# Talking-heads attention and two feed-forward layers: softmax statistics for two chunks at a time, one pair of heads of values and scores in every step, and 64-column scores

## The chip, the cores and the metric

One core of a Trainium2 chip. The time is device microseconds of one execution. An execution under the profiler gives a trace besides, with its span: from the first to the last instruction of the program.

## What is computed

Talking-heads attention over 2 batches, 12 heads, 448 positions and 64 features, then two gated feed-forward layers over the 896 tokens, all in float32:

```python
scores = scale * np.matmul(q, k.transpose(0, 1, 3, 2))
scores = np.einsum('bhij,hg->bgij', scores, w_pre)
scores = scores - np.max(scores, axis=-1, keepdims=True)
attn = np.exp(scores)
attn = attn / (np.sum(attn, axis=-1, keepdims=True) + 1e-09)
attn = np.einsum('bhij,hg->bgij', attn, w_post)
return np.matmul(attn, v).astype(np.float32)
...
g = x @ w_gate
silu = g * (1.0 / (1.0 + np.exp(-g)))
val = x @ w_val
return (silu * val @ w_out).astype(np.float32)
...
h = x @ w_in
relu6 = np.clip(h + 3.0, 0.0, 6.0)
g = h * relu6 / 6.0
return (g @ w_out).astype(np.float32)
```

The heads are mixed before the softmax (`w_pre`) and after it (`w_post`).

## The kernel before

The attention is cut into 8 tiles `t` of queries, 4 for each batch (`TILES`, lines 34 to 37), and each tile into chunks of 10 queries: 12, 12, 12, 9, 11, 12, 12 and 10 chunks, 90 in all. A step `i` of the main loop (lines 553 to 585, 45 steps) works on two chunks. Since the stages of a chunk pair run in different steps, each step issues work of several pairs.

- `scores` (line 154) makes the scores of one pair of heads for a whole tile, with the queries as the stationary operand in two groups of rows: 64 and the rest. The rest is `n - 64`, with `n` ten times the number of chunks: 56 columns for 12 chunks, 46 for 11, 36 for 10, and 26 for tile 3, which has 9. Each of the two heads gets a PSUM bank of the tag `pqk`, which has two. `scores_out` (line 177) copies them into one of two score buffers in SBUF, `Ss[t % 2]`. `qk` (line 500) is both.
- `relayout` and `relayout_rest` (lines 186 and 201) move the score rows of a chunk, by DMA, into a tile `sx` in which the heads lie on partitions. The large part is issued on SP's queue, the small one on POOL's. A pool of 5 holds `sx`. A tile's rows can be moved when all six pairs of heads of that tile have been copied, and its score buffer can be written again when all of its rows have been read.
- `premix` (line 210) mixes the heads of two chunks on TensorE, 8 instructions, into two banks of the tag `ppre`, which has four. It runs two steps ahead (`LOOK`).
- `row_max`, `exps` and `weights` (lines 228 to 246) work on one chunk each: the negated maximum of each row on VectorE; the exponential with its row sum on ScalarE; the sum plus 1e-9, its reciprocal, and `w_post` times the reciprocal on VectorE.
- `postmix` (line 248) mixes the heads again on TensorE, 64 instructions for two chunks, into the two banks of the tag `ppost`. `attn_out` (line 269) copies one bank with VectorE and the other with ScalarE into `at`.
- `av` (line 287) multiplies one pair of heads of a tile with the values, in one `pqk` bank. `x_out` (line 308) copies it into a staging tile; for tiles 6 and 7 `x_last` (line 328) casts it on ScalarE and subtracts on VectorE. `x_split` runs on POOL.

The order of the work is written out by hand; each engine executes its instructions in that order. Lines 506 to 509 place the scores of tiles 2 to 7: tile 2 in steps 2 to 7, tile 3 in 8 to 13, tile 4 in 13 to 17 (two in step 13), then 19 to 24, 24 to 29, 30 to 35. Lines 512 to 518 place `av`, two pairs of heads in one step, three such steps for each tile. Before the loop the scores of tiles 0 and 1 are made. Weights of the first two feed-forward products are loaded and converted during steps 20 to 35 on ScalarE and VectorE, and begun on TensorE in the last steps (`fill`).

A step issues, in this order: `postmix(i)`; both `exps` of pair `i + 1`; `attn_out(i)`; `weights` of its first chunk; the scores of this step and their copies; `weights` of its second chunk; `premix(i + 2)` and both `row_max`; `av`; and `x_out` with loads, conversions and relayouts.

After the loop come the six `av` of tile 7 (line 587), which take banks of `ppre` and `ppost` in turn, and the feed-forward layers (lines 654 to 670): 52 pairs of PSUM banks, given out in a fixed rotation (`BANKS`, line 341).

## Time and profile before

| | |
|---|---|
| median of 3 runs | 710.16 us (709.96 to 710.25) |
| span of the profiled execution | 712.3 us |
| TensorE matmuls busy | 679.8 us (95%) |
| VectorE busy | 517.3 us (73%) |
| ScalarE busy | 303.1 us (43%) |
| GpSimd busy | 147.9 us (21%) |

The span is 2.1 us above the median; no time of its own is given for the profiled execution. Busy is the union of an engine's instructions. PE is TensorE, DVE VectorE, ACT ScalarE, POOL GpSimd, SP the queue that issues most DMAs; L259 is line 259 of the kernel. The ends of matmuls are modelled, and one may be drawn as long while it waits. Steps can be found in the trace by their `postmix`: step 9 starts at 57.10 us, 13 at 78.88, 14 at 85.89, 36 at 174.93 and 44 at 203.84. The feed-forward products proper begin at 219.90.

### The profile page before, as it was taken

How to read it: one execution, taken by the hardware profiler on the slowest of the kernel's cores; microseconds unless marked ns; L12 is line 12 of the kernel's file. 1: busy time of each engine (PE TensorE's matmuls, PEld its weight loads, DVE VectorE, ACT ScalarE, POOL GpSimd, SP SyncE). 2: the span in 40 equal slices, each digit the busy share in tenths (PEclk: the TensorE clock that was granted, in tenths of full speed). 3: DMA queues.
4: the chain of work that ended last, by engine and by line, in shares of the span. 5: the costliest groups of instructions: out<-in, count | busy, mean ns of one | idle time of the engine just before them, and what ended most of it. 6: DMA issues, size and time to landing. Idle time of an engine off the chain costs nothing.

```text
span 712.3 us, 16449 instructions
## 1 busy us (share of the span) xinstructions
PE 679.8 (95%) x6864; PEld 570.3 (80%) x6864; DVE 517.3 (73%) x925; ACT 303.1 (43%) x581; POOL 147.9 (21%) x185
## 2 busy tenths in 40 slices
PE   9698899899879999999999999999999999999997
PEld 3353465565569999999999999999999999999997
DVE  4785578899845888888878666568888888764650
ACT  4574566667533424334343322324544544333320
POOL 2422244442420121131112000002332332000000
PEclk9999999999999999999999999999999999999999
DMA  5777346443421424333342334223323323544420
GB/s 193 219 207 210 110 123 193 141 160 100 125 87 46 133 91 133 105 117 114 109 126 97 108 114 133 89 89 94 128 90 95 126 82 97 166 145 144 136 71 27
DMA packets 33628, 86.73 MB, mean 122 GB/s; under 512 B 9265, under 2 KB 21953, under 8 KB 33553
## 3 DMA queue, kind: packets, MB, share of 16 engines
q1 hardware_dynamic: 25632, 80.97, 35.4%
q0 software_dynamic: 7200, 3.94, 2.4%
q8 instruction: 54, 0.88, 0.5%
q10 hardware_dynamic: 720, 0.77, 0.3%
q14 instruction: 22, 0.17, 0.1%
HBM read 62.20 MB, written 2.75 MB: 91 GB/s over the span
## 4 chain that ended last, share of the span: by engine, by line
PE 83%; DVE 8%; DMA 4%; ACT 2%; issue 2%; SPq 0%; POOL 0%; ACTq 0%; DVEq 0%; POOLq 0%
PE pi L394 16%; PE pp L394 16%; PE po L394 12%; PE pg L394 12%; PE pv L394 12%; PE pav L295 4%; PE pqk L166 4%; PE ppost L259 3%; DMA sx<-S 2%; DVE nm L230 2%; PE ppre L217 2%; DVE wn L245 2%; DMA q<-in_q_dram 2%; DVE at L283 1%; ACT e L236 1%
## 5 line engine op out<-in xcount | busy, mean ns | idle before, releaser
L394 PE MATMUL pp<-g,hp 128*128 128x448 f32 x384 | 109.1, 365 | 0.0
L394 PE MATMUL po<-u,ho 128*128 128x448 f32 x288 | 81.7, 364 | 0.0
L259 PEld LDWEIGHTS ppost<-wn,e 60*64 60x64 f32 x2880 | 49.5, 136 | 37.5 <-ACT at L283 12.8
L605 POOL TENSOR_TENSOR g<-rl,g 128x448 fp32r<-128x448 f32 x32 | 41.6, 1319 | 169.0 <-ACT g L604 169.0
L394 PEld LDWEIGHTS pp<-g,hp 128*128 128x128 f32 x384 | 72.0, 187 | 5.8
L236 ACT ACTIVATE e<-ppre,nm 128x448 f32<-128x448 f32 x90 | 56.2, 630 | 47.8 <-DVE nm L230 47.6
L206 POOL DMA_DIRECT2D sx<-S x90 | 52.1, 579 | 110.5 <-ACT S L182 37.2
L259 PE MATMUL ppost<-wn,e 60*64 60x60 f32 x2880 | 55.8, 223 | 16.6 <-DVE rc L242 5.5
L394 PE MATMUL pi<-x2h,li 128*128 128x448 f32 x192 | 70.2, 366 | 0.0
L394 PE MATMUL pi<-x2l,hi 128*128 128x448 f32 x192 | 70.0, 364 | 0.0
L394 PE MATMUL pi<-x2h,hi 128*128 128x448 f32 x192 | 69.9, 364 | 0.0
L394 PE MATMUL pp<-g,lp 128*128 128x448 f32 x192 | 69.3, 361 | 0.0
L605 POOL TENSOR_TENSOR u<-sg,u 128x448 fp32r<-128x448 f32 x24 | 32.6, 1378 | 152.7 <-ACT u L604 152.7
L230 DVE TENSOR_REDUCE nm<-ppre 128x1 f32<-128x448 f32 x90 | 51.7, 616 | 9.0 <-PE ppre L217 9.0
L394 PEld LDWEIGHTS po<-u,ho 128*128 128x128 f32 x288 | 54.1, 188 | 3.8
L166 PE MATMUL pqk<-k,q 64*64 64x448 f32 (+4 forms) x384 | 53.3, 567 | 3.4 <-ACT S L182 1.9
L295 PEld LDWEIGHTS pav<-at,v 128*64 128x64 f32 x768 | 36.9, 137 | 23.4 <-ACT S L182 17.6
L394 PE MATMUL po<-u,lo 128*128 128x448 f32 x144 | 52.3, 363 | 0.0
L394 PE MATMUL pg<-xl,hg 128*128 128x448 f32 x138 | 50.5, 366 | 0.0
L394 PE MATMUL pv<-xl,hv 128*128 128x448 f32 x138 | 50.5, 366 | 0.0
L394 PE MATMUL pg<-xh,hg 128*128 128x448 f32 x138 | 50.5, 366 | 0.0
L394 PE MATMUL pv<-xh,hv 128*128 128x448 f32 x138 | 50.4, 365 | 0.0
(105 smaller groups left out, 1359.3 us busy)
## 6 DMA issues: line engine op xcount, KB each, us to landing
sx<-S SPq DMA_DIRECT2D x90, 182.0 KB
ri<-in_moe_w_in_dram SPq DMA_DIRECT2D x16, 768.0 KB
rg<-in_moe_w_gate_dram SPq DMA_DIRECT2D x12, 768.0 KB
rv<-in_moe_w_val_dram SPq DMA_DIRECT2D x12, 768.0 KB
ro<-in_moe_w_out_dram SPq DMA_DIRECT2D x12, 768.0 KB
rp<-in_moe_w_out_dram SPq DMA_DIRECT2D x12, 640.0 KB
rp<-in_moe_w_out_dram SPq DMA_DIRECT2D x6, 768.0 KB
sx<-S POOLq DMA_DIRECT2D x90, 42.0 KB, 5.0
```

Of the source, the lines that this page charges most:

```text
L166: nc.tensor.matmul(p[e][lo:hi, :S], lhsT=qs[b][r, base + lo : base + hi], rhs=ks[b][r, c, :], start=True, stop=True, tile_position=(64 * e ...
L206: nc.gpsimd.dma_start(out=sx[m // 2][104:128, m % 2, :], in_=rows[8:, :H, :])
L217: nc.tensor.matmul(p[a][64 * r : 64 * r + 64, :S], lhsT=W1[rows, :], rhs=x[rows, r, :], start=True, stop=True, tile_position=(64 * a, 64 * r),
L230: nc.vector.tensor_reduce(nm, pre[m][:, :S], AX.X, ALU.max, negate=True)
L236: nc.scalar.activation(e[:, :S], pre.pop(m)[:, :S], AF.Exp, bias=tot.pop(m), scale=1.0, accum_out=sm)
L245: nc.vector.tensor_scalar(wn, W2, rc, None, ALU.mult)
L259: nc.tensor.matmul(p[s][64 * c : 64 * c + 64, r, b, :, :], lhsT=e[rows, k0 : k0 + 64], rhs=wn[rows, :, :], start=True, stop=True, tile_pos ...
L283: copy(dst, p[r].rearrange("p a b h k -> p a (b h) k"))
L295: nc.tensor.matmul(p[64 * e : 64 * e + 64, :n], lhsT=vs[b][:, jc, h, :], rhs=ats[t][:, jc, h, :n], start=jc == 0, stop=jc == JC - 1, tile_ ...
L394: nc.tensor.matmul(p[:, :S], lhsT=wt[:, kk, :], rhs=xx, start=start, stop=stop)
L605: eng.tensor_tensor(to[1], src, to[0].bitcast(F32), ALU.subtract)
```

## The change

- The two chunks of a pair share one `ppre` tile of two banks. One instruction takes both maxima, one adds 1e-9, one takes both reciprocals, and one tensor-tensor multiply makes the weights of both, with `w_post` and the reciprocals broadcast.
- The scores of tiles 2 to 7 are placed one pair of heads in each of the steps 1 to 36, at the end of the step, after `premix`. `av` comes right after `exps`, one pair of heads in each of the steps 6 to 40 (two in step 18) and six in steps 41 to 44.
- `x_out` runs on ScalarE, between `attn_out` and `weights`. Of the score copies VectorE does the first head's always (before, not for odd pairs from tile 2 on).
- In tile 3 the second group of score rows has 64 columns in place of 26: it reads on into the next queries, 40 zero columns are appended to `q`, and the additional rows are not used.
- The feed-forward layers take pairs of banks in the rotation `pqk`, `ppre`, `ppost`, `ppre`, a `ppre` pair being one tile; the six `av` of tile 7 take `ppost` alone.

```diff
-    BUFS = {"pqk": 2, "ppre": 4, "ppost": 2}
+    BUFS = {"pqk": 2, "ppre": 2, "ppost": 2}
+
+    def two_banks(name, tag):
+        if tag == "ppre":
+            p = ps.tile([128, 2, 512], F32, name=name, tag=tag, bufs=BUFS[tag])
+            return [p[:, a, :] for a in range(2)]
+        return [ps.tile([128, 512], F32, name=f"{name}_{a}", tag=tag, bufs=BUFS[tag]) for a in range(2)]
...
-            lo, hi = 64 * s, min(64 * s + 64, n)
+            lo, hi = 64 * s, 64 * s + (64 if n < 97 else min(64, n - 64 * s))
...
-            copy = nc.scalar.copy if e or (t > 1 and c % 2) else nc.vector.tensor_copy
+            copy = nc.scalar.copy if e else nc.vector.tensor_copy
...
+    def row_max(i):
+        nm = pe.tile([128, 2], F32, name=f"nm{i}", tag="nm", bufs=3)
+        nc.vector.tensor_reduce(nm, pre[i][:, :, :S], AX.X, ALU.max, negate=True)
+        tot[i] = nm
+
+    def exps(i):
+        p, nm = pre.pop(i), tot.pop(i)
+        sm = pe.tile([128, 2], F32, name=f"sm{i}", tag="sm", bufs=3)
+        e2 = [es[(2 * i + a) % 6] for a in range(2)]
         for a in range(2):
...
+            nc.scalar.activation(
+                e2[a][:, :S], p[:, a, :S], AF.Exp, bias=nm[:, a : a + 1], scale=1.0, accum_out=sm[:, a : a + 1]
+            )
+        ew[i] = (e2, sm)
+
+    def weights(i):
+        sm = ew[i][1]
+        rc = pe.tile([128, 2], F32, name=f"rc{i}", tag="rc", bufs=3)
         nc.vector.tensor_scalar(rc, sm, 1e-9, None, ALU.add)
         nc.vector.reciprocal(rc, rc)
...
+        wn = pe.tile([128, 2, GP], F32, name=f"wn{i}", tag="wn", bufs=3)
+        w2 = W2.rearrange("p g k -> p (g k)")
+        nc.vector.tensor_tensor(
+            wn, w2.unsqueeze(1).to_broadcast([128, 2, GP]), rc.unsqueeze(2).to_broadcast([128, 2, GP]), ALU.mult
+        )
...
-        nc.vector.tensor_copy(stage[t][:, c, :n], pavs.pop((t, c))[:, :n])
+        nc.scalar.copy(stage[t][:, c, :n], pavs.pop((t, c))[:, :n])
...
-    for t, (begin, end) in enumerate(((2, 7), (8, 13), (13, 17), (19, 24), (24, 29), (30, 35)), 2):
+    for t in range(2, 8):
         for c in range(HP):
-            at_step(begin + c * (end - begin + 1) // HP, qk, t, c, place="qk")
-        scored[t] = end
+            at_step(6 * t - 11 + c, qk, t, c, place="qk")
+        scored[t] = 6 * t - 6
...
-    for t in range(7):
-        begin = (first[t + 1] - 1) // 2 + 1
-        end = first[t + 2] // 2 - 1 if t < 6 else NP - 1
+    for t, (begin, end) in enumerate(((6, 11), (12, 17), (18, 22), (23, 28), (29, 34), (35, 40), (41, 44))):
         for c in range(HP):
-            i = begin + (c // 2) * (end - begin) // 2
+            i = begin + c * (end - begin + 1) // HP
             at_step(i, av, t, c, place="av")
-            at_step(i, x_out if t < 6 else x_last, t, c)
+            at_step(i, x_out if t < 6 else x_last, t, c, place="out")
...
-        soft = [2 * (i + 1) + a for a in range(2)] if 0 <= i + 1 < NP else []
-        for m in soft:
-            exps(m)
+        soft = 0 <= i + 1 < NP
+        if soft:
+            exps(i + 1)
+        run(i, "av")
         if i >= 0:
             attn_out(i)
-        for m in soft[:1]:
-            weights(m)
-        run(i, "qk")
-        for m in soft[1:]:
-            weights(m)
+        run(i, "out")
+        if soft:
+            weights(i + 1)
         if i + LOOK < NP:
             premix(i + LOOK)
-            for a in range(2):
-                row_max(2 * (i + LOOK) + a)
+            row_max(i + LOOK)
         if i >= NP - 3:
             fill(FILL[i - NP + 3])
-        run(i, "av")
+        run(i, "qk")
...
-        av(7, c, ("ppre", "ppost")[c % 2])
+        av(7, c, "ppost")
...
+        part.append(np.zeros((128, QPAD), q.dtype))
```

## Rows read from the trace of the kernel before

**Rows 1.** Busy time by stretches: stretch, its length, then busy us of each engine.

```profile
65.00:67.19 2.19, 0.07 (x6) 0.05 (x4) 0.58 (x2) 1.34 (x4) 1.14 (x2) 1.00 0.86 228
67.19:70.60 3.41, 3.41 (x28) 0.84 (x28) 1.65 (x7) 0.64 (x1) 1.15 (x2) 0.50 0.84 221
...
85.89:174.93 89.04, 80.45 (x2149) 51.95 (x2141) 75.95 (x239) 59.26 (x147) 34.55 (x56) 1.00 0.47 148
174.93:203.84 28.91, 23.47 (x703) 17.06 (x703) 23.94 (x82) 17.37 (x47) 12.75 (x19) 1.00 0.46 138
203.84:219.90 16.06, 14.07 (x224) 12.35 (x223) 4.45 (x10) 2.38 (x9) 1.80 (x1) 1.00 0.01 2
...
240.00:270.00 30.00, 30.00 (x149) 27.80 (x148) 25.26 (x32) 12.74 (x20) 5.55 (x4) 1.00 0.38 125
```

After the length stand PE, PE's weight loads, DVE, ACT and POOL, then the granted clock, the share of DMA and GB/s.

**Rows 2.** The chain of waits that ended last: start us, us, what.

```profile
78.95 1.09 PE ppost L259 x64
...
163.72 0.48 ACT e L236
164.26 0.81 ACT e L236 x3
165.06 0.53 ACT at L283
165.59 0.40 ACT S L182
166.03 1.75 PE pav L295 x32
```

**Rows 3.** Timeline of TensorE: start us, us, what (steps 9 and 25).

```profile
57.10 1.16 PE L259 MATMUL ppost<-wn,e 60*64 60x60 f32 x64
58.08 1.79 PE L166 MATMUL pqk<-k,q 64*64 64x448 f32 x8
...
132.60 0.93 PE L166 MATMUL pqk<-k,q 64*64 64x448 f32 x8
133.35 0.93 PE L217 MATMUL ppre<-sx,W 64*64 64x448 f32 x8
```

**Rows 4.** Groups of TensorE's score matmuls by form: busy us, mean ns of one.

```profile
L166 PE MATMUL pqk<-k,q 64*26 64x448 f32 x24 | 6.3, 603 | 0.0
...
L166 PE MATMUL pqk<-k,q 64*36 64x448 f32 x24 | 5.5, 535 | 0.0
```

**Rows 5.** Groups of VectorE from 17 to 221 us: busy us, mean ns of one.

```profile
L230 DVE TENSOR_REDUCE nm<-ppre 128x1 f32<-128x448 f32 x90 | 51.7, 616 | 9.0 <-PE ppre L217 9.0
L283 DVE COPY at<-ppost 128x480 f32<-128x480 f32 x45 | 30.1, 670 | 15.0 <-PE ppost L259 15.0
L245 DVE TENSOR_SCALAR wn<-W,rc 128x60 f32<-128x60 f32 x90 | 27.6, 307 | 3.1
L243 DVE RECIPROCAL rc<-rc 128x1 f32<-128x1 f32 x90 | 14.8, 164 | 3.1
L242 DVE TENSOR_SCALAR rc<-sm 128x1 f32<-128x1 f32 x90 | 12.7, 142 | 0.3 <-ACT e L236 0.3
...
L334 DVE TENSOR_TENSOR xl<-pav,xh 128x120 fp32r<-128x120 f32 (+1 forms) x12 | 3.1, 268 | 11.1 <-ACT xh L333 11.1
```

**Rows 6.** Groups of ScalarE from 17 to 221 us.

```profile
L333 ACT CAST xh<-pav 128x120 fp32r<-128x120 f32 (+1 forms) x12 | 3.0, 251 | 12.5 <-PE pav L295 12.5
```

**Rows 7.** Timelines of ScalarE and VectorE: in brackets the idle time before, and who ended it.

```profile
31.77 0.53 ACT L182 COPY S<-pqk 120x448 f32<-120x448 f32 x1 [1.84 <-DMA sx<-S]
...
54.78 0.62 DVE L182 COPY S<-pqk 90x448 f32<-90x448 f32 x1 [1.77 <-DMA sx<-S]
```

**Rows 8.** DMA issues on POOL's queue, us to landing: from 80 to 195, from 44 to 62.

```profile
sx<-S POOLq DMA_DIRECT2D x54, 42.0 KB, 4.6
...
sx<-S POOLq DMA_DIRECT2D x9, 42.0 KB, 7.0
```

**Rows 9.** The chain of waits again, at the DMA ahead of tile 3's scores.

```profile
45.65 7.14 DMA sx<-S
```

More of the change, by code (lines that the diff above doesn't have):

```diff
@@ L38 @@
 SQ = 45 * KI
+QPAD = 40
 WARM = (7, 17)
@@ L97, in new_qk @@
     def new_qk(b):
-        qs[b] = big.tile([128, HP * SQ], F32, name=f"q{b}", tag="big")
+        qs[b] = big.tile([128, HP * SQ + QPAD], F32, name=f"q{b}", tag="big")
         ks[b] = big.tile([128, HP, S], F32, name=f"k{b}", tag="big")
@@ L102, in load_q @@
         lo, hi = (HP * KI * sum(c for _, _, c in TILES[b][:i]) for i in (i0, i1))
+        if i1 == 4:
+            hi += QPAD
         nc.sync.dma_start(out=qs[b][:, lo:hi], in_=qT[b, :, lo:hi])
@@ L160, in scores @@
         base = HP * KI * sum(x for _, _, x in TILES[b][:i]) + c * n
-        p = [ps.tile([128, 512], F32, name=f"pqk{t}_{c}_{e}", tag=tag, bufs=BUFS[tag]) for e in range(2)]
+        p = two_banks(f"pqk{t}_{c}", tag)
         for s in range(2):
-            lo, hi = 64 * s, min(64 * s + 64, n)
+            lo, hi = 64 * s, 64 * s + (64 if n < 97 else min(64, n - 64 * s))
             for e in range(2):
@@ L212, in premix @@
         x = sx.pop(i)
-        p = [ps.tile([128, 512], F32, name=f"ppre{i}_{a}", tag="ppre", bufs=BUFS["ppre"]) for a in range(2)]
+        p = ps.tile([128, 2, 512], F32, name=f"ppre{i}", tag="ppre", bufs=BUFS["ppre"])
         for r in range(2):
@@ L217, in premix @@
                 nc.tensor.matmul(
[L218 removed]
+                    p[64 * r : 64 * r + 64, a, :S],
                     lhsT=W1[rows, :],
@@ L224, in premix @@
                 )
[L225 to L241 removed]
+        pre[i] = p
+    def row_max(i):
[6 more added lines that the diff above has]
+        e2 = [es[(2 * i + a) % 6] for a in range(2)]
+        for a in range(2):
+            nc.scalar.activation(
[5 more added lines that the diff above has]
+        rc = pe.tile([128, 2], F32, name=f"rc{i}", tag="rc", bufs=3)
         nc.vector.tensor_scalar(rc, sm, 1e-9, None, ALU.add)
         nc.vector.reciprocal(rc, rc)
[L244 to L246 removed]
+        wn = pe.tile([128, 2, GP], F32, name=f"wn{i}", tag="wn", bufs=3)
[3 more added lines that the diff above has]
+        )
+        wns[i] = wn
     def postmix(i):
@@ L251, in postmix @@
         ]
+        e2, wn = ew.pop(i)[0], wns.pop(i)
         for r in range(2):
-            e, wn = ew.pop(2 * i + r)[0], wns.pop(2 * i + r)
+            e = e2[r]
             for b in range(JC):
@@ L261, in postmix @@
                             lhsT=e[rows, k0 : k0 + 64],
-                            rhs=wn[rows, :, :],
+                            rhs=wn[rows, r, :].rearrange("p (g k) -> p g k", k=KG),
                             start=True,
@@ L339, with pair_of_banks @@
     HALVES = [(0, S), (S, S)]
-    BANKS = ["pqk", "ppre", "ppost", "ppre", "pqk", "ppre", "ppost", "ppre"]
-    turn = [0]
-    def bank(name):
-        tag = BANKS[turn[0] % 8]
+    TURNS = ["pqk", "ppre", "ppost", "ppre"]
+    turn = [2]
+    def pair_of_banks(name):
+        tag = TURNS[turn[0] % 4]
         turn[0] += 1
-        return ps.tile([128, 512], F32, name=name, tag=tag, bufs=BUFS[tag])
-    def pair_of_banks(name):
-        return [bank(f"{name}_{hf}") for hf in range(2)]
+        return two_banks(name, tag)
     def load_w(pool, src, kc, name):
@@ L460, in first_products @@
         for j in range(2):
-            begun[j] = bank(f"p0_{j}")
-            yield from product_half(begun[j], whl[j], 0, 6, 6, of_x, 0)
+            if j == 0:
+                begun[j] = [ps.tile([128, 512], F32, name="p0_0", tag="pqk", bufs=BUFS["pqk"])]
+            else:
+                begun[j] = two_banks("p0_1", "ppre")
+            yield from product_half(begun[j][0], whl[j], 0, 6, 6, of_x, 0)
     def keep_clock(n):
@@ L488 @@
     new_v(0)
-    extra = {i: {"qk": [], "av": [], "end": []} for i in range(-LOOK, NP)}
+    extra = {i: {"qk": [], "av": [], "out": [], "end": []} for i in range(-LOOK, NP)}
     def at_step(i, f, *args, place="end"):
@@ L665 @@
         if k0 == 0:
-            pp = [begun[j], bank(f"p{kind}{idx}_1")] if j < 2 else pair_of_banks(f"p{kind}{idx}")
+            if j == 0:
+                begun[j].append(ps.tile([128, 512], F32, name="p0_0b", tag="pqk", bufs=BUFS["pqk"]))
+            pp = begun[j] if j < 2 else pair_of_banks(f"p{kind}{idx}")
         product(pp, whl.pop(j), k0, kc, count[kind], operand[kind], fillers if j < 2 else None)
```

17 lines of the change are left out of this document (removed).

## The prediction

> **What bounds the kernel now.** I read the busy time by stretches first. From 219.90 us on the products of the two feed-forward layers run: in 240 to 270 us TensorE is busy for all of the 30 us [rows 1], and the change leaves those products alone, so nothing can be won there. All of the change lies before 219.90 us, in the 45 attention steps. Of the 89.04 us from step 14 to step 36 TensorE counts 80.45 as busy and VectorE 75.95 [rows 1]: two engines close to full, neither full, which is the picture of engines that wait for each other.
>
> The chain of waits shows whose turn ends last [rows 2]. At step 33 it goes through ScalarE: the two exponentials (163.72 to 165.06, 1.34 us), the copy of the mixed weights (0.53 us), the copy of a score (0.44 us until TensorE has it), and only then the two products with the values (1.75 us, so 0.87 for each pair of heads). `av` waited there for a PSUM bank which a score held. Steps with values do two pairs at once, and the steps between do none.
>
> TensorE's own price of a step's parts is read from starts: the second mix 0.98 us (57.10 to 58.08), scores of 56 columns 0.75 us (132.60 to 133.35), the first mix, of the same shape, as much [rows 3]. Scores of tile 3 take 1.79 us where those of 56 columns take 0.93 [rows 3]; by form, the 26-column ones have a mean of 603 ns, the 36-column ones 535 [rows 4].
>
> **The change part by part.** *Narrow scores.* Six calls at 0.86 us more than the wide form [rows 3]: 5.2 us on TensorE. The first is covered by a DMA wait (below), so 4.3 us can be won; it is not added by itself, since the steps below are priced with the wide form. The rows give a width at which it is slow, not a reason. The Trainium skill (TensorEngine Tiling (Array Packing), Key Properties) says that a change of tiling mode drains the array, and column tiles exist at 32 and at 64. By that rule a 26-column matmul is another mode than its neighbours, one of 36 is not, and the change takes the whole difference; the trace agrees so far, and by the rule alone rival B would have no chance.
>
> *One maximum, one reciprocal, one multiply.* Means of one, VectorE [rows 5]: before, two maxima 1.23, two sums, reciprocals and multiplies 2 x (0.142 + 0.164 + 0.307) = 1.23, mixed copy 0.67. After: a maximum over two banks is not in the trace; it lies between 0.62 (one) and 1.23 (two), and streams as many elements as two, so I take two less the cost of an operation on one column, 1.23 - 0.14 = 1.09. The multiply becomes a tensor-tensor over 120 columns: the subtraction of that shape takes 0.268 [rows 5]; bounds 0.25 and 0.61 (two of the old). So 0.142 + 0.164 + 0.268 = 0.57. VectorE saves 0.8 us a step.
>
> What it costs is order: the first exponential now waits for both maxima and the multiply for both exponentials. The loop maximum, exponentials, weights, next maximum is 1.09 + 1.34 + 0.57 + about 0.2 for three hand-overs (estimate) = 3.2 us. Before, the second exponential overlapped the second maximum; so no step can now be shorter than 3.2, also where TensorE has only 2.5 to 2.6 us to do.
>
> *The moved steps.* On TensorE each step is now second mix, `av`, first mix, scores: 0.98 + 0.87 + 0.75 + 0.75 = 3.35 us. `x_out`'s 36 copies go from VectorE to ScalarE, at 0.25 us each (the cast of the same shape [rows 6]); 18 score copies go the other way, 0.62 each [rows 7]. VectorE's step is 0.67 + 0.57 + 1.09 + 0.62 = 2.95 us. Queued on ScalarE are now score copy, two exponentials, mixed copy, `x_out`. The scores have two banks, one of which `av` held, so they wait for `x_out`, and the next score copy for the scores: 0.44 + 1.34 + 0.53 + 0.25 + 0.93 = 3.5 us [rows 2, 3, 6]. That is the longest of the four loops and gives a step with both kinds of work: **3.5 us**. Bounds: 3.35 (TensorE alone) and 3.9 (no overlap at all between neighbours on ScalarE).
>
> *Where it starts.* Tile 2's scores move from step 2 to step 1, tile 3's from step 8 to 7, at the step's end. Their copies may only overwrite the score buffer when its relayout DMAs have read it, and they waited for that: at 31.77 us (1.84 us) and 54.78 us (1.77 us) [rows 7]. Those DMAs are issued in the same order and not earlier, so the copies still begin near 31.8 and 54.7. Behind them on ScalarE and VectorE now stand the next exponentials and weights. From 54.7: copy 0.44, exponentials 1.34, weights 0.57 and hand-overs put the second mix of step 9 at 57.2, against 57.10 [rows 3]. So up to step 9: 0 us (-1 to +3); the later first weights (about 1 us, from the loop above) vanish in the same wait.
>
> *Steps 9 to 13* took 57.10 to 78.9 [rows 2, 3], 21.8 us. Now 4 x 3.5 = 14.0, plus a TensorE stall of 2.1 us that no engine released (65.00 to 67.19) and the stretch at half clock, 1.2 GHz, behind it (67.19 to 70.60) [rows 1], which costs half its length at most, taken as 1.5: 17.6. **-4.2.**
>
> *Steps 13 to 36* took 96.0 us, 4.2 a step. Now 23 x 3.5 = 80.5, plus 6.5 for weight conversions, another such stall and unevenness (0.28 a step, estimate), plus late relayouts. These have two steps from the last score of tiles 4 to 7 to the first mix that needs them: two steps, less the score copy behind the scores, leave 3.5 + 1.85 - 1.0 = 4.35 us. The small relayout on POOL's queue is issued 0.4 after the copy and lands 4.6 later (median of 80 to 195 us), 7.0 in 44 to 62 us [rows 8]: late by 0.65, three times, 2.0 in all (0 to 9). 89.0. **-7.0.**
>
> *Steps 36 to 44* took 28.9 [rows 1]. One step with scores 3.5, seven at the 3.2 loop 22.4, the stall 2.1, early products and one late relayout 1.3: 29.3. **+0.4.**
>
> *The end* took 16.06 [rows 1]. One wait of `av` for a bank, some 0.7, goes; the last six `av` on two banks: an `av` of 0.87, then cast 0.25 and subtraction 0.27, just fit the next one's 0.87. **-0.7.** The feed-forward part has four pairs of banks in turn as before: 0.
>
> Sum: 0 - 4.2 - 7.0 + 0.4 - 0.7 = -11.5 us. The profiled span is 712.3, 2.1 over the median of the runs, 710.16; what lies around it I take as unchanged. 710.2 - 11.5 = **698.7 us**.
>
> One price stays outside the sum. While copies wait for DMAs until 31.8 and 54.7, TensorE stands still longer than before; at 65 to 67 us it did so and the granted clock was 0.50 after it [rows 1]. The Trainium skill (TensorE: Matmul & The Clock Gate, Part 1) says that throttled is the default state and activity releases it. By that rule step 8 would be followed by one more half-clock stretch, at 1.7 us at most (half of 3.41), and the time would be 700.4.
>
> **The rivals.**
> A, TensorE sets the pace: score copies and `x_out` fit between, steps 9 to 36 take 3.35, relayouts are in time: 27 x 0.15 + 2.6 = 7 less, **692**. For it: at 80.45 of 89.04 TensorE is the fullest engine. Against: the chain at step 33 runs through ScalarE.
> B, the change doesn't do all it says: the narrow scores stay slow for a cause other than width, five calls x 0.86: **703**.
> C, ScalarE's loop overlaps less: 3.8 a step, 27 x 0.3 = 8 more: **707**. For it: ScalarE has no slack at 3.5.
> D, **slower**: late relayouts. At the first mix of steps 20, 26, 32 and 38 TensorE, and all behind it, waits for the score rows of the next tile. The large relayout has no landing in the view; the one issued at 45.65 held a copy until 54.78, 9.1 us [rows 7, 9]. If that is what it takes, each tile waits 9.1 - 4.35 = 4.75, four tiles 19, in place of the 2.6 in the sum: 698.7 + 16.4 = **715**. It decides from a landing of 8 us on (4.35 + 14.1 / 4). Against: it was measured while queries and keys were loaded as well; later the small ones land in 4.6, not 7.0.
>
> **How the numbers follow.** The forecast (695 to 702) has 0.50, A 0.15, B 0.10, C 0.10, D 0.10, and 0.05 that gains and losses cancel. About 0.2%, 1.4 us, is what a measurement of this kernel can tell from no change. Forecast, A, B and C are faster: 0.85; 0.05 within; D slower: 0.10. The range takes in A with 2 us below it and C with 2 us above, 690 to 709; D, the cancelling case and the tails are left out.
>
> **What would show it.** Tile 3's scores at 0.93 us; one maximum at 1.09 and one multiply near 0.27; from step 13 on, starts of the second mix 3.5 to 3.9 apart with one `av` in each; the chain from score copy over exponentials and `x_out` to the scores. Wrong would be: step 9 well after 57 us; the first mix of steps 20, 26, 32, 38 released by a relayout more than 2 us late; steps of 4 us with ScalarE or VectorE always busy; a maximum near 1.5 us, which alone lengthens the 3.2 loop past 3.5.

## The result and the profile after

The changed kernel takes **715.16 us**, the one before 709.18 us (medians of 16 runs each): a ratio of 1.0087 [1.0061, 1.0112], slower, where 698.7 us was predicted and 709 was the end of the range. The three runs shown ahead of the prediction (median 710.16) were a close group by chance: 16 runs of the kernel before lie between 704.35 and 714.18, those of the changed one between 712.26 and 717.72. Ratios here and below compare the runs that lie within 1.5% of the fastest of their kernel; slower ones are left out (4 of 12 for `shared_only`, at most two of any comparison for the kernel before).

The profiled execution of the changed kernel took 715.27 us, with a span of 713.5, so 1.8 us lie around the span; in the timed runs of the kernel before it is 1.7 to 1.9. The span of before was 712.3, so that its profiled execution took some 714 us (estimate from these): 5 us more than the median, and not 2 below its own span.

The two profiles by stretches. The first numbers of a line are the start and end in us, then the length, then the busy time (and instructions) of TensorE, its weight loads, VectorE, ScalarE and GpSimd, the granted clock, and the share and rate of the DMAs. First the changed kernel: steps 14 to 36, 36 to 44, step 44 to the feed-forward products, the third kind of feed-forward product (`pi`), and the last (`pp`).

```profile
77.74:166.74 89.00, 85.77 (x2133) 60.46 (x2129) 69.11 (x140) 56.24 (x157) 34.20 (x57) 0.98 0.51 154
166.74:199.86 33.12, 28.68 (x746) 20.04 (x738) 21.27 (x48) 18.81 (x54) 13.49 (x20) 1.00 0.39 121
199.86:212.88 13.02, 13.02 (x208) 11.60 (x207) 2.25 (x7) 2.10 (x7) 1.09 (x1) 1.00 0.01 3
468.59:590.49 121.90, 119.47 (x577) 107.23 (x575) 99.25 (x104) 53.53 (x88) 36.17 (x28) 1.00 0.27 90
591.13:709.15 118.02, 116.32 (x576) 107.69 (x576) 67.62 (x90) 34.41 (x52) 5.08 (x4) 1.00 0.37 115
```

And the `pi` stretch of the kernel before:

```profile
475.18:592.07 116.89, 116.89 (x578) 108.36 (x577) 99.55 (x107) 55.20 (x92) 36.64 (x29) 1.00 0.30 99
```

The reader is to see two things. Between these two profiles the attention became shorter: the feed-forward products begin at 212.88 us instead of 219.90 [rows 1], 7.0 earlier. But the profile of before was a long one: in two kernels below that have the old order and the narrow scores (`before_pad`, `before_pair_ff`) they begin at 215.0 and 210.4, so these 7.0 us are no measure of the change. The part which the change was said to leave alone became longer: TensorE, which was busy for all of `pi` before, now stands still for 2.4 of 121.90 us, and `pi` takes 5.0 us more. From the first feed-forward product to the last, before took 488.7 us (219.9 to 708.6), after 496.3 (212.88 to 709.15): **+7.6**.

By step (starts of the second mix), in us:

| stretch | before | after | predicted |
|---|---|---|---|
| start to step 9 | 57.10 | 59.23 | 57.1 |
| 9 to 13 | 21.8 | 14.3 | 17.6 |
| 13 to 36 | 96.0 | 93.2 | 89.0 |
| 36 to 44 | 28.9 | 33.1 | 29.3 |
| 44 to the feed-forward products | 16.1 | 13.0 | 15.4 |
| feed-forward products | 488.7 | 496.3 | 488.7 |

Where the 7.6 us arise is in the chain of waits (start, length, engine, tile and line). Before, TensorE stood alone in it from the first of these products to the last; of the changed kernel:

```profile
382.35 86.40 PE po L407 x432
468.75 14.66 PE pi L407 x72
...
483.43 0.96 DVE li L398
...
492.26 0.96 DVE li L398
493.22 1.06 DVE rl L641 x2
```

From 483 us on VectorE carries the chain, with the conversion of the next weights (`yi`, `li`) and the gate (`rl`). The timelines of ScalarE and VectorE there say why; the bracket at the end of a line is the idle time before an instruction and what ended it.

```profile
499.78 0.63 ACT L640 ACTIVATE rl<-pi,half 128x448 f32<-128x448 f32 x1
501.49 0.63 ACT L640 ACTIVATE rl<-pi,half 128x448 f32<-128x448 f32 x1 [1.08 <-DVE rl L641]
```

```profile
499.91 0.96 DVE L398 TENSOR_TENSOR li<-yi,hi 128x768 fp32r<-128x768 f32 x1 [0.90 <-ACT hi L396]
500.79 0.61 DVE L641 SCALAR_TENSOR_TENSOR rl<-rl,pi 128x448 f32<-128x448 f32 x1
502.16 0.62 DVE L641 SCALAR_TENSOR_TENSOR rl<-rl,pi 128x448 f32<-128x448 f32 x1 [0.76 <-ACT rl L640]
...
508.74 0.96 DVE L398 TENSOR_TENSOR li<-yi,hi 128x768 fp32r<-128x768 f32 x1 [0.90 <-ACT hi L396]
```

A product has two halves, in two PSUM banks. ScalarE reads a half (`Relu`, L640), VectorE multiplies it (L641). In the changed kernel a `ppre` pair is one tile of two banks, and ScalarE's read of the second bank waits 1.08 us until VectorE has read the first; VectorE then waits 0.76 for ScalarE. From one `li` to the next the two engines take 7.65 us where the pair is two tiles (492.26 to 499.91) and 8.83 where it is one (499.91 to 508.74). The Trainium skill (PSUM — Partial Sum Buffer, PSUM bank collisions raise a hardware error) says that two engines reading one bank at once collide, that the compiler's scheduler keeps them apart with a dependency, and that accesses to different banks run clean. The banks here differ, and the wait was there all the same: it ended with VectorE's read of the other bank of the same tile (`<-DVE rl L641`), so in this program the readers are ordered by the tile.

In the attention steps, VectorE's and ScalarE's groups from 17 to 215 us (busy us and mean ns of one, then idle time before them):

```profile
L238 DVE TENSOR_REDUCE nm<-ppre 128x2 f32<-128x896 f32 x45 | 49.0, 1089 | 20.7 <-PE ppre L226 20.6
L258 DVE TENSOR_TENSOR wn<-W,rc 128x120 f32<-128x120 f32 x45 | 14.1, 312 | 1.5
L254 DVE TENSOR_SCALAR rc<-sm 128x2 f32<-128x2 f32 x45 | 8.4, 186 | 12.7 <-ACT e L246 12.7
```

```profile
L329 ACT COPY xs<-pav 128x120 f32<-128x120 f32 (+2 forms) x36 | 9.4, 262 | 0.5 <-PE pav L311 0.5
```

The maximum takes 1089 ns (1.09 predicted), the weights 0.19 + 0.17 + 0.31 = 0.66 us (0.57), `x_out` 262 ns (0.25). The maximum and `x_out` held; the weights were 0.09 us dearer.

### The profile page after: what moved, and what is told of

Same layout as the page of the kernel before. It is cut to its first block, busy times and chain, and to the rows that moved or that the text cites. A ratio compares the mean times of both kernels' runs of the same rounds, so it can differ in the third digit from the quotient of the medians.

```text
span 713.5 us, 16198 instructions
## 1 busy us (share of the span) xinstructions
PE 688.0 (96%) x6864; PEld 582.6 (82%) x6864; DVE 501.7 (70%) x727; ACT 298.0 (42%) x599; POOL 147.3 (21%) x185
## 4 chain that ended last, share of the span: by engine, by line
PE 74%; DVE 17%; ACT 4%; DMA 2%; issue 2%; SPq 0%; ACTq 0%
PE pp L407 14%; PE po L407 12%; PE pv L407 11%; PE pg L407 11%; PE ppost L275 5%; PE pav L311 5%; PE pqk L175 5%; PE ppre L226 5%; DVE yi L385 3%; DVE yi L382 2%; PE pi L407 2%; DMA sx<-S 2%; DVE li L398 2%; DVE rl L641 2%; DVE yi L388 2%
## 5 line engine op out<-in xcount | busy, mean ns | idle before, releaser
L275 PEld LDWEIGHTS ppost<-wn,e 60*64 60x64 f32 x2880 | 56.9, 139 | 32.8 <-issue 14.6
L275 PE MATMUL ppost<-wn,e 60*64 60x60 f32 x2880 | 58.3, 224 | 10.5 <-DVE wn L258 5.7
L617 POOL TENSOR_TENSOR u<-sg,u 128x448 fp32r<-128x448 f32 x24 | 33.1, 1401 | 152.4 <-ACT u L616 152.4
L238 DVE TENSOR_REDUCE nm<-ppre 128x2 f32<-128x896 f32 x45 | 49.0, 1089 | 20.7 <-PE ppre L226 20.6
L226 PE MATMUL ppre<-sx,W 64*64 64x448 f32 x360 | 52.5, 583 | 3.6 <-DMA sx<-S 3.2
L175 PE MATMUL pqk<-k,q 64*64 64x448 f32 (+3 forms) x384 | 53.1, 575 | 0.5 <-ACT S L191 0.4
L407 PE MATMUL pg<-xh,hg 128*128 128x448 f32 x132 | 48.5, 367 | 0.0
L407 PE MATMUL pv<-xh,hv 128*128 128x448 f32 x132 | 48.5, 367 | 0.0
L407 PE MATMUL pv<-xh,lv 128*128 128x448 f32 x132 | 48.4, 367 | 0.0
L407 PE MATMUL pg<-xh,lg 128*128 128x448 f32 x132 | 48.4, 367 | 0.0
```

The source lines that it names most:

```text
L175: nc.tensor.matmul(p[e][lo:hi, :S], lhsT=qs[b][r, base + lo : base + hi], rhs=ks[b][r, c, :], start=True, stop=True, tile_position=(64 * e ...
L226: nc.tensor.matmul(p[64 * r : 64 * r + 64, a, :S], lhsT=W1[rows, :], rhs=x[rows, r, :], start=True, stop=True, tile_position=(64 * a, 64 * r),
L238: nc.vector.tensor_reduce(nm, pre[i][:, :, :S], AX.X, ALU.max, negate=True)
L275: nc.tensor.matmul(p[s][64 * c : 64 * c + 64, r, b, :, :], lhsT=e[rows, k0 : k0 + 64], rhs=wn[rows, r, :].rearrange("p (g k) -> p g k", k=KG),
L407: nc.tensor.matmul(p[:, :S], lhsT=wt[:, kk, :], rhs=xx, start=start, stop=stop)
L617: eng.tensor_tensor(to[1], src, to[0].bitcast(F32), ALU.subtract)
```

## The experiments

Every kernel was timed in five rounds beside the kernel before. A ratio is to that one, whose median stands behind the slash; the ratio is the one on record and can differ from the quotient of the two medians by up to 0.3%. Each kernel below has 6 to 12 runs. They were timed in four groups on three chips, and the kernel before had a median of 708.69 to 709.38 us in three of them and of 705.21 in that of the last two kernels: between groups, ratios are compared and not times.

### The pair that is one tile

**ff_single**: the changed kernel, with `ppre` pairs as two tiles from the end of the attention on.

```diff
+        if tag == "ppre" and ffp:
+            return [ffp[0].tile([128, 512], F32, name=f"{name}_{a}", tag=tag, bufs=4) for a in range(2)]
...
+    att.close()
+    ffp[0] = ctx.enter_context(tc.tile_pool(name="psf", bufs=4, space=PSUM))
     fill(FILL[3])
```

> The changed kernel, with the feed-forward layers alone back on single PSUM banks. Theory (a pair of banks in one tile puts ScalarE's read of the second bank behind VectorE's read of the first, and every second product of the third kind then runs at 8.8 us instead of 7.7): the feed-forward part takes 489 us again instead of 496, the whole some 7.5 us less than the changed kernel, 707 to 709. Rival (the 40 columns more in the q tiles move the other tiles in SBUF, and matmuls or VectorE read more slowly there): no change, 715. Rival (weights arrive late): no change, 715.

706.51 / 709.38, ratio 0.9965 [0.9939, 0.9992]: from slower to a little faster by this edit alone. The `pi` stretch is back at 117.29 us with a busy TensorE, and ScalarE's two reads follow each other:

```profile
466.51:583.80 117.29, 117.29 (x578) 108.29 (x577) 99.92 (x108) 55.44 (x92) 37.04 (x29) 1.00 0.30 99
```

```profile
504.16 1.16 ACT L647 ACTIVATE rl<-pi,half 128x448 f32<-128x448 f32 x2
```

Beside this kernel the feed-forward part of the changed one is 8.0 us longer in the profiles (496.3 against 488.3): `pi` takes 4.6 more, and the other 3.4 lie behind it, where the first products of `pp` wait for weights that VectorE, still behind, has not converted. The stretch of `pp` here, with a TensorE that never stops, against the 118.02 above:

```profile
583.63:699.01 115.38, 115.38 (x577) 107.81 (x575) 64.53 (x86) 32.26 (x48) 4.41 (x4) 1.00 0.36 114
```

**before_pair_ff**: the kernel before, with nothing of the change but these pairs and what goes with them, the rotation of the pairs and the last six `av` on two banks.

```diff
...
+    def two_banks(name, tag):
+        if tag == "ppre":
+            p = ffp[0].tile([128, 2, 512], F32, name=name, tag=tag, bufs=2)
+            return [p[:, a, :] for a in range(2)]
...
```

> The kernel before with only the pairs of banks in the feed-forward layers as the change has them (one tile for a ppre pair, and the last six products with values on two banks). Theory: 7 us slower, 716 to 717, all of it in the products of the third kind, at 8.8 us for every second one. Rival (placement, late weights): 709, unchanged.

718.20 / 709.38, ratio 1.0116 [1.0080, 1.0152]: +8.2 us by itself. Not all of it lies in `pi`, as was expected: that stretch takes 5.3 us more (122.24 against 116.89), and from its end to the last product it is 3.4 more (119.9 against 116.5). The same wait is there:

```profile
465.72:587.96 122.24, 119.43 (x577) 107.34 (x575) 99.62 (x104) 53.54 (x88) 36.53 (x28) 1.00 0.27 90
```

```profile
498.70 0.64 ACT L639 ACTIVATE rl<-pi,half 128x448 f32<-128x448 f32 x1 [1.08 <-DVE rl L640]
```

**ff_grouped**: the pairs stay one tile; ScalarE's two reads are issued ahead of VectorE's two, so that the engines change places once and not three times (the first kind of product, with its `Sigmoid`, is edited in the same way).

```diff
...
+            rls = [scratch(f"rl{idx}_{hf}") for hf in range(2)]
+            for hf in range(2):
+                nc.scalar.activation(rls[hf], pp[hf][:, :S], AF.Relu, bias=half, scale=1.0 / 6.0)
             for hf in range(2):
-                sg = scratch(f"rl{idx}_{hf}")
-                nc.scalar.activation(sg, pp[hf][:, :S], AF.Relu, bias=half, scale=1.0 / 6.0)
+                sg = rls[hf]
```

> The changed kernel, pairs of banks and all, with one edit: in the first and third kind of product ScalarE's reads of both banks are issued ahead of VectorE's two. Theory (in a pair an engine's read waits for the other engine's read ahead of it in the program): ScalarE's second read no longer waits 1.1 us, VectorE's first waits some 0.6 us for it instead, so about half of the loss comes back, 710 to 712. Rival (the pair costs by being given back only when both halves are read): 715, unchanged.

708.75 / 708.69, ratio 1.0002 [0.9970, 1.0034]. VectorE's two multiplies now stand together, and the loss is gone with the tile unchanged: it is the alternation of two readers on one tile that costs, not the tile's size. The expected half was too little: in the profile `pi` is as short as in `ff_single` and the feed-forward part takes 488.7 us (488.3 there, 496.3 in the changed kernel). By the ratios 6.0 of the 8.6 us are back; the rest is less than these runs can tell.

```profile
498.40 1.14 DVE L643 SCALAR_TENSOR_TENSOR rl<-rl,pi 128x448 f32<-128x448 f32 x2
```

```profile
474.65:591.94 117.29, 117.29 (x578) 108.29 (x577) 99.62 (x107) 55.53 (x91) 37.42 (x28) 1.00 0.29 96
```

### The parts of the attention

**before_wide**: the kernel before, with the 64-column scores and the padding of `q` alone.

```diff
...
-            lo, hi = 64 * s, min(64 * s + 64, n)
+            lo, hi = 64 * s, 64 * s + (64 if n < 97 else min(64, n - 64 * s))
...
```

> The kernel before with only the 64-column scores of tile 3, and the zero columns that they read. If they are worth what the prediction gave them: 4 to 5 us less, 704 to 705. If SBUF placement matters, the feed-forward part runs at another pace here than in the kernel before (7.36 instead of 7.30 us for 36 matmuls) and takes back 2 us or more.

704.51 / 709.38, ratio 0.9936 [0.9898, 0.9974]: -4.5 us, with 4.3 in the prediction's working. That a gain is there is clear of the interval, its size is not (1.8 to 7.2 us), and the profiles show less: the steps 8 to 13, which hold tile 3's scores, take 29.1 us here and 30.2 in `wide_loads_moved`, against 30.8 and 31.5 in `before_pair_ff` and `before_pad` with the narrow ones. Scores by form: 24 of the 64-column ones are new, and the 603 ns of the 26-column ones [rows 4] are gone.

```profile
L169 PE MATMUL pqk<-k,q 64*64 64x448 f32 x168 | 35.8, 544 | 3.7 <-ACT S L185 1.9 <-issue 1.7
L169 PE MATMUL pqk<-k,q 64*36 64x448 f32 x24 | 5.5, 535 | 0.0
```

The rule of the Trainium skill that the prediction weighed (TensorEngine Tiling (Array Packing), Key Properties: a change of tiling mode drains the array) agrees with this gain; no run isolates a drain.

**before_pad**: the kernel before with `q` tiles 40 columns longer, which nothing reads.

```diff
...
-        qs[b] = big.tile([128, HP * SQ], F32, name=f"q{b}", tag="big")
+        qs[b] = big.tile([128, HP * SQ + QPAD], F32, name=f"q{b}", tag="big")
```

> The kernel before with nothing but 40 unused columns more in the q tiles, so that the tiles of the same pool lie 160 bytes further apart in SBUF. If placement sets the pace of the feed-forward matmuls: 36 matmuls of the first two kinds at 7.36 instead of 7.30 us, the third part at 86.5 instead of 87.5, and the whole within 1 us of the kernel before, 708 to 710. If not, the paces of the kernel before, and the change of pace in the wide kernel has another cause.

707.76 / 708.97, ratio 0.9976 [0.9944, 1.0008]. The work is the same, and only the place of other tiles in SBUF can have changed, yet the pace of the products is another (more in the last section). In the profile that comes to 0.4 us of the feed-forward part; the interval leaves 0 to 4 us for the whole, so how much of the gain of `before_wide` is due to the columns alone isn't shown.

**all_single**: the changed kernel with `ppre` as four single banks everywhere and so two maxima of one bank each; sums, reciprocals and multiply stay shared.

```diff
...
-        nc.vector.tensor_reduce(nm, pre[i][:, :, :S], AX.X, ALU.max, negate=True)
+        for a in range(2):
+            nc.vector.tensor_reduce(nm[:, a : a + 1], pre[i][a][:, :S], AX.X, ALU.max, negate=True)
...
```

> The changed kernel with single PSUM banks everywhere and so two maxima, one for each bank; the shared reciprocal and multiply, the order and the wide scores stay. Theory: the feed-forward part at 489 us as in the run before this one, and an attention part as fast or up to 3 us faster, since the first exponential waits for one maximum only: 704 to 708. If the shared maximum were worth what the change put it in for, this would be 2 to 4 us slower than with single banks in the feed-forward layers alone.

705.26 / 709.38, ratio 0.9940 [0.9911, 0.9970]. Beside `ff_single` (0.9965, one maximum in the attention) the shared maximum gains nothing that shows: two of one bank take 1.15 us together here, the shared one 1.09, and the first exponential waits for all of it. Step 0, which holds neither scores nor values, takes 2.63 us here and 3.19 in the changed kernel.

**order_only**: `all_single` with a sum, a reciprocal and a multiply for each chunk, so that of the change only the new order, the moved copies, the wide scores and the rotation of the feed-forward pairs are left (the sums of a pair, and its weights, still share one tile).

```diff
...
+        for a in range(2):
+            rc = pe.tile([128, 1], F32, name=f"rc{i}_{a}", tag="rc", bufs=6)
+            nc.vector.tensor_scalar(rc, sm[:, a : a + 1], 1e-9, None, ALU.add)
+            nc.vector.reciprocal(rc, rc)
+            nc.vector.tensor_scalar(wn[:, a, :], w2, rc, None, ALU.mult)
...
```

> Single banks everywhere, two maxima, and the sum, reciprocal and multiply of each chunk by themselves as before: of the change only the order of the steps, x_out on ScalarE and the wide scores are left. If sharing reciprocal and multiply is worth its 0.6 us a step: VectorE's step grows from 3.0 to 3.5 us and the loop with it, 4 us or more above the run with all banks single (705.3), 709 to 711. If TensorE and ScalarE set the step anyway: 705 to 707.

709.42 / 708.69, ratio 1.0005 [0.9966, 1.0044]. Against `before_wide`, which has the old order and the same scores, the order by itself loses 1.0005 - 0.9936, some 4.9 us of 709; the two intervals just overlap. The expectation had VectorE lengthen every step of the loop, and that is not what the profile shows: steps 9 to 13 take 14.26 us, exactly as in `all_single`, and 13 to 36 are no longer (93.6 against 95.5). The loss lies in steps 36 to 44, which hold no scores but one: 36.2 us, against 32.1 in `all_single` and 26.3 to 30.2 in five profiles with the old order.

**shared_only**: the reverse, `before_wide` with shared sum, reciprocal and multiply in the old order.

```diff
...
-        for m in soft[:1]:
-            weights(m)
         run(i, "qk")
-        for m in soft[1:]:
-            weights(m)
+        if soft:
+            weights(i + 1)
...
```

> The kernel before with the wide scores (704.5 us) and the shared sum, reciprocal and multiply, in the old order. VectorE saves 0.6 us a step. If steps without values wait for VectorE, as their 2.6 us suggests: 5 us less, 699 to 701. If the wait for both exponentials takes the place of what is saved: 704 to 707.

705.47 / 708.69, ratio 0.9927 [0.9884, 0.9969], against 0.9936 without it: nothing that shows, with intervals of 0.4% to either side (by the medians of all runs it is 0.9955). In the new order the shared weights are worth some 4.6 us (0.9940 against 1.0005, with intervals that just overlap), in the old one no gain shows: as far as these runs can tell, they repair the new order.

### Where the new order loses time

From step 13 to 36 the changed kernel's steps took 93.2 us, 12.45 of them for two, 24 to 26; the 21 others average 3.85 (predicted 3.5 plus 0.28 for unevenness). In step 24 the chain goes through a relayout, and the queue of SP shows what stood ahead of it:

```profile
111.74 0.93 PE ppre L226 x8
...
113.68 0.71 SPq L208
...
114.43 8.07 DMA sx<-S
...
122.55 1.01 PE ppre L226 x2
```

```profile
108.03 1.74 SPq L208 DMA_DIRECT2D sx<-S  x1
109.81 2.12 SPq L121 DMA_DIRECT2D v<-in_v_dram  x1
111.98 0.66 SPq L367 DMA_DIRECT2D rg<-in_moe_w_gate_dram  x1
112.80 2.32 SPq L208 DMA_DIRECT2D sx<-S  x2
```

The first mix of pair 26, whose chunks lie inside tile 4, waits for a relayout issued behind a load of values (384 KB) and one of weights (768 KB); it lands 8.1 us after its issue, and the granted clock is 0.50 for 3.4 us after that stop (122.3 to 125.7). This is not one execution alone: TensorE waits for a relayout between 112 and 130 us in all eight profiles that have the new order, tile 4's scores in six steps and these loads where the change has them (0.8 to 4.2 us), and in none with the old order. The stretch after the stop, with the granted clock third from the end:

```profile
122.30:125.70 3.40, 3.15 (x26) 1.35 (x28) 1.09 (x1) 0.00 (x0) 0.00 (x0) 0.50 0.16 56
```

**score_lead**: `ff_single` with the scores of tiles 4 to 7 in five steps, which gives their relayouts a step more.

```diff
...
-            at_step(6 * t - 11 + c, qk, t, c, place="qk")
-        scored[t] = 6 * t - 6
+            at_step(6 * t - 11 + (c if t < 4 else c * 5 // HP), qk, t, c, place="qk")
+        scored[t] = 6 * t - (6 if t < 4 else 7)
...
```

> On top of single banks in the feed-forward layers (706.5 us): tiles 4 to 7 get their scores in five steps instead of six, two pairs of heads in the first one, so that their relayouts can start a step earlier, as before the change. Theory (late relayouts cost the steps around 19, 22 to 25, 28, 39 and 40 some 6 to 8 us): steps 18 to 41 lose at least half of that, 702 to 704, and the first mix waits for no relayout there. Rival (relayouts queue behind the weight and value loads, whenever they are issued): 705 to 707.

706.29 / 708.97, ratio 0.9947 [0.9918, 0.9975]; `ff_single` had 0.9965. TensorE's waits for relayouts fall from 2.3 to 0.6 us, but a step with two pairs of scores takes 5.2 to 6.0 us, because the second pair waits for the first pair's copies (5.1 us in all, 3.3 in `ff_single`): what one wait gave the other took, and no gain shows.

**tile2_later**: `ff_single` with tile 2's scores in steps 2 to 7, as before.

```diff
...
-            at_step(6 * t - 11 + c, qk, t, c, place="qk")
-        scored[t] = 6 * t - 6
+            at_step(6 * t - 11 + c + (t == 2), qk, t, c, place="qk")
+        scored[t] = 6 * t - 6 + (t == 2)
...
```

> On top of single banks in the feed-forward layers (706.5 us): tile 2's scores in steps 2 to 7 as before the change, not in 1 to 6. Theory (their copies, queued a step earlier, hold the exponentials behind them until the relayouts of tile 0 have landed, and the ninth step starts 3 us later than before): step 9 starts at 56 to 57 us instead of 58.5, the whole 704 to 705. Rival (the start is set by the loop over the shared maximum, 3.2 us a step instead of 2.8): step 9 not before 58 us, 706 to 707.

708.93 / 708.97, ratio 0.9999 [0.9968, 1.0030], no better than `ff_single`. Step 3 begins 4.6 us earlier (32.11 against 36.75), and step 9 begins at 59.10 all the same (58.53): the loss by tile 2's place fell as a theory. Nor is it the loop over the shared maximum, the rival, since `all_single` has two maxima and reaches step 9 at 59.90. What sets the start isn't shown.

**last_after**: `ff_single` with `x_last` of tile 6 behind the weights. In the changed kernel VectorE's subtraction stands ahead of them and waits for ScalarE's cast:

```profile
194.03 0.28 DVE L350 TENSOR_TENSOR xl<-pav,xh 128x120 fp32r<-128x120 f32 x1 [1.09 <-ACT xh L349]
194.23 0.16 DVE L254 TENSOR_SCALAR rc<-sm 128x2 f32<-128x2 f32 x1
...
194.63 0.28 DVE L258 TENSOR_TENSOR wn<-W,rc 128x120 f32<-128x120 f32 x1
```

```diff
...
-            at_step(i, x_out if t < 6 else x_last, t, c, place="out")
+            at_step(i, x_out if t < 6 else x_last, t, c, place="out" if t < 6 else "last")
...
```

> On top of single banks in the feed-forward layers (706.5 us): tile 6's cast and subtraction (x_last) are issued after the weights instead of before them, in steps 41 to 44. Theory (they stand in the loop maximum, exponentials, copy, cast, subtraction, weights, and the steps with them take 4.0 to 4.8 us instead of 3.6): 0.7 us less in each of four steps, 703 to 704. Rival (these steps are long because of late relayouts alone): no change, 706.5.

706.74 / 708.97, ratio 0.9967 [0.9931, 1.0003]: no change to the whole. The mechanism is there, the subtraction now follows the weights without a wait, and steps 41 and 42 take 3.68 and 3.71 us in place of 4.31 and 3.99; but in the profile step 43 took 5.60 (4.79 in `ff_single`), and the 0.9 us don't show.

```profile
190.64 0.28 DVE L263 TENSOR_TENSOR wn<-W,rc 128x120 f32<-128x120 f32 x1
190.88 0.28 DVE L355 TENSOR_TENSOR xl<-pav,xh 128x120 fp32r<-128x120 f32 x1
```

**combined**: `all_single`, with `x_last` behind the weights and the scores of tile 7 alone one step ahead.

```diff
...
-            at_step(6 * t - 11 + c, qk, t, c, place="qk")
-        scored[t] = 6 * t - 6
+            at_step(6 * t - 11 + (c if t < 7 else c * 5 // HP), qk, t, c, place="qk")
+        scored[t] = 6 * t - (6 if t < 7 else 7)
...
```

> All banks single, x_last after the weights, and tile 7 alone scored a step earlier, so that the relayouts ahead of steps 39 and 40 come in time. If the ends of the attention part are what the new order loses (some 3 us in steps 36 to 44): 702 to 703, the fastest so far. If the doubled step of tile 7 takes back what the earlier relayouts give: 705.

704.45 / 708.69, ratio 0.9935 [0.9900, 0.9971], against 0.9940 of `all_single`. Steps 36 to 44 take 28.97 us in its profile, as in the kernel before (32.05 in `all_single`, 33.12 in the changed kernel), but the whole gains nothing that shows. Two waits of the first mix for relayouts are left (total, number, longest, in us):

```profile
PE ppre L223 <- DMA sx<-S: 1.5, 2, 1.3
```

**loads_moved**: `combined`, with the values of the second batch loaded in steps 13 to 16 (16 to 22 before) and the first weights in step 16 (20), so that none of it stands in SP's queue ahead of the relayouts that step 24 needs.

```diff
...
-    at_step(16, new_v, 1)
+    at_step(13, new_v, 1)
-        at_step(16 + 2 * j, load_v, 1, j)
+        at_step(13 + j, load_v, 1, j)
-        at_step(20 + 8 * j, fetch, j, "early")
+        at_step((16, 28)[j], fetch, j, "early")
...
```

> The combined version (704.5 us) with the second batch's values loaded in steps 13 to 16 and the first weights in step 16, ahead of tile 4's relayouts instead of among them. Theory (those relayouts are late because they queue behind 384 and 768 KB of loads): steps 24 to 29 lose their 4 to 5 us of excess, 700 to 702, the fastest. Rival (the loads delay tile 3's relayouts instead, or the lateness comes from the short lead alone): 704 to 706.

700.11 / 705.21, ratio 0.9917 [0.9887, 0.9948], the lowest ratio of all (the kernel before, too, was 3.5 us shorter in this group than in `combined`'s). The value and weight loads now go out by 86 us, no first mix waits for a relayout between 112 and 130 us, and the step from 24 to 25 takes 3.54 us (6.05 in `combined`). Steps 24 to 29 lose 2.5 us together, not the expected 4 to 5.

```profile
83.93 1.42 SPq L118 DMA_DIRECT2D v<-in_v_dram  x1
85.40 1.24 SPq L365 DMA_DIRECT2D rg<-in_moe_w_gate_dram  x1
```

**wide_loads_moved**: the same loads moved in `before_wide`, the old order.

```diff
...
-    at_step(16, new_v, 1)
+    at_step(13, new_v, 1)
...
-        at_step(20 + 8 * j, fetch, j, "early")
+        at_step((16, 28)[j], fetch, j, "early")
...
```

> The kernel before with the wide scores (704.5 us) and the same two loads moved. Theory: the old order gives its relayouts one step more of lead and they are not late there, so nothing changes, 704 to 705. If it gains as much as the new order does, the loads cost something else than late relayouts.

706.75 / 705.21, ratio 0.9992 [0.9965, 1.0018]: nothing gained. In the profiles of the old order no first mix waited for a relayout in these steps, so the place of the loads is a price of the new one. The ratio is 0.0056 above that of `before_wide`: either the move costs the old order some 4 us, or the wide scores gave less in this group. `before_wide` was not run in it, so this stays open.

The best version, `loads_moved`, beats the changed kernel clearly. Its interval meets those of `combined` and `before_wide`, so that it is better than the wide scores alone isn't shown.

## Why the prediction was wrong

The sum failed at three of its terms, and the price of a step came out by luck.

**"The feed-forward part has four pairs of banks in turn as before: 0"** is the step that turned the sign. Measured: +8.2 us alone (`before_pair_ff`), -8.6 when taken out (`ff_single` against the changed kernel), 7.6 between the profiles. In its place the runs showed that ScalarE waits 0.9 to 1.1 us for VectorE in seven of the eight `ppre` pairs of `pi`. The working counted banks and their turn and did not ask who reads them. The diff turns two tiles into one, and in the feed-forward part two engines read such a pair alternately. It was in view: VectorE was busy for 99.6 of the 116.9 us of `pi` before, so an added wait of 1.1 and 0.8 us in every second product could not be hidden for long. None of the rivals was of this kind. Rival D forecast the right time, 715, by a mechanism that accounts for little of it: with the pairs as two tiles and the late relayouts still there (`ff_single`) the kernel is no slower than before. That its number fits is luck.

**The base: "2.1 over the median ... what lies around it I take as unchanged."** A run of the kernel before takes 1.7 to 1.9 us more than its span, so the profiled execution lay some 5 us above the median, and its surplus lay in the attention. Steps 9 to 13, 21.8 us there, held a stop of TensorE that no engine released and a stretch at half clock [rows 1]; the same steps take 17.8 and 18.8 in `before_pair_ff` and `before_pad`, with the same order and scores. "-4.2" for them was counted as won by the change, and the larger part of it was no price of the old order. By the medians the attention gained little: the kernel's +6.0 less the 7.6 to 8.6 of the feed-forward part leaves some -2 us, in place of -11.5.

**"36 to 44: +0.4"** measured +4.2 in the profile. The seven steps "at the 3.2 loop" took 3.0 to 5.1 (the loop itself was priced well: step 0, which holds neither scores nor values, took 3.19; that step 37 took 2.96 shows that it is no floor): the steps 41 to 44 hold `x_last` in `x_out`'s place, ahead of the weights, and the step charged neither the wait for ScalarE's cast nor the relayouts at 38 to 40. With both mended and single banks the stretch took 28.97 (`combined`).

**"13 to 36": -7.0** measured -2.8. 12 of the 23 steps lie between 3.5 and 3.8, as priced. "2.0 for late relayouts", with 0 to 9 as bounds, was too little: the prediction took the small relayout on POOL's queue for the one that matters and left SP's queue out, where the loads of values and weights stand ahead of the large one. It landed 8.1 us after its issue, close to rival D's point of decision of 8, but for a pair inside tile 4; of D's four places only step 38 shows a wait of TensorE, 0.9 us. One profile does not give the size of the term: kernels with the new order and the scores in the same steps took 90.1 to 97.0 us there.

**The step of 3.5 us** came out, but not by the loop that it was read from. The prediction had ScalarE's loop as the longest, at 3.5, and TensorE at 3.35. In the profile the chain of waits from 59 to 74 and from 139 to 160 us runs through TensorE alone, which goes from part to part without a stop, while ScalarE waits 1.1 us in each step for the scores. The chain over score copy, exponentials and `x_out`, which was to show the loop, isn't there:

```profile
62.82 1.11 PE L275 MATMUL ppost<-wn,e 60*64 60x60 f32 x64
63.86 1.04 PE L311 MATMUL pav<-at,v 128*64 128x120 f32 x16
64.83 0.98 PE L226 MATMUL ppre<-sx,W 64*64 64x448 f32 x8
65.64 0.96 PE L175 MATMUL pqk<-k,q 64*64 64x448 f32 x8
66.39 1.13 PE L275 MATMUL ppost<-wn,e 60*64 60x60 f32 x64
```

```profile
66.68 0.53 ACT L191 COPY S<-pqk 90x448 f32<-90x448 f32 x1 [1.11 <-PE pqk L175]
```

From start to start, second mix, `av`, first mix and scores take 1.04 + 0.97 + 0.81 + 0.75 = 3.57 us; the prediction had read 0.98, 0.87, 0.75 and 0.75 from the kernel before. So it is rival A's mechanism, at a price that both A and the forecast had too low, and that it meets ScalarE's 3.5 is luck. It also says why less work on VectorE wins nothing in these steps (`order_only`).

**What was right.** The wide scores gain, against rival B, although the 4.5 us that stand beside the 4.3 have an interval of 1.8 to 7.2 and the profiles show less. The maximum at 1.09, `x_out` at 0.25. The start: 0 with bounds of -1 to +3 against +2.1. Less well: the weights, 0.57, took 0.66, and the end gained 3.0 us where 0.7 were predicted. The further half-clock stretch behind step 8, which the prediction left outside its sum, didn't come: the granted clock was 1.00 from 50 to 70 us. It came in step 24 instead, behind the stop for the relayout.

**Open.** Runs of one kernel spread over 4 to 10 us. The profiles hold different amounts of stops of TensorE that no engine released (0.4 us in the attention of `before_pair_ff`, 6.6 in that of `all_single`), which may be part of it; no run says what makes them. Nor does any say what sets the start of step 9, which lies between 55.6 and 59.9 us in the profiles.

## What to carry to other kernels

When a diff changes what a tile is, follow every place that takes the tile's tag, and ask in each which engines read it in turn: two banks in one tile cost `pi` nothing where one engine read both ahead of the other (`ff_grouped`), and a wait per hand-over where the two alternated. Make the sum against a typical execution: set the profiled time, not its span, beside several runs, and don't book a stall of that execution as a gain of the change. And an even order of work gives a gain only if every DMA on its way arrives in time, so look at what stands ahead of it in the same queue. A step that takes as long as forecast does not show the forecast's reason: look which engine waits in it and which never does.

## What the runs showed of the hardware

The pace of the float32 products changes when tiles in SBUF are made longer. With 40 unused columns appended to two tiles and no other edit (`before_pad`), 36 matmuls of the first kinds take 7.36 us where they took 7.30, 432 of `po` take 86.40 in place of 87.36, and 576 of `pp` 115.23 in place of 116.49. The chains of `before_pad` and of the kernel before, with start and length in us:

```profile
369.77 7.36 PE pg L395 x36
...
384.49 86.40 PE po L395 x432
588.02 115.23 PE pp L395 x576
```

```profile
373.38 7.30 PE pg L394 x36
...
387.98 87.36 PE po L394 x432
...
592.07 116.49 PE pp L394 x576
```

From `po` on, the products end after 318.9 us (384.33 to 703.23) in place of 320.7, but those ahead of it take 1.4 us more, so that of the whole feed-forward part 0.4 us are left (488.2 against 488.7). That it is the place of the tiles behind the longer ones is the likely reason, as nothing else differs; no run varies the place by itself. In the experiments above, the kernels with a padded `q` and single banks show the 86.40 and the 115.23 as well. So parts of a kernel can differ by 1 to 2 us for a reason that is no part of its order.

Appended columns, a changed tile, a moved copy: the parts moved the time by 0 to 8 us, no more than runs of one kernel spread, and only the intervals over many runs and the stretches of the profile could tell them apart.
